# Two attentions on one core: the first step's scores moved into the projections' last turn, and a pair of maxima moved inside each output product

## The chip, the cores and the metric

One Trainium2 chip, one core of it. The number that counts is the device time of one execution in microseconds (us); a kernel's time is the median of its runs. The core has five engines that work side by side and meet through semaphores: TensorE (PE in the profile, with its weight loads shown apart as PEld), VectorE (DVE), ScalarE (ACT), GpSimd (POOL) and SyncE (SP, which here only issues DMAs).

## The reference: what is computed

Two multi-head attentions over a sequence of 2048 with 576 channels, 32 heads of 18 channels, each with its own input and weights. A attends to 8 earlier positions at a stride of 2; B is full softmax attention. Both end in a 576 x 576 output product, and the two results stand side by side.

```python
def _A_ref(x, wqkv, wo):
    qkv = (x @ wqkv).reshape(B, S, 3, H, Dh).transpose(2, 0, 3, 1, 4)
    q, k, v = qkv[0], qkv[1], qkv[2]
    idx = pos[:, None] - (jnp.arange(8) * 2)[None, :]          # masked where negative
    logits = einsum("bhsd,bhswd->bhsw", q, k[:, :, idx]) * Dh ** -0.5
    o = einsum("bhsw,bhswd->bhsd", softmax(logits), v[:, :, idx])
    return o.transpose(0, 2, 1, 3).reshape(B, S, D) @ wo
def _B_ref(x, wqkv, wo):
    q, k, v = ...                                              # as above
    p = softmax(einsum("bhqd,bhkd->bhqk", q, k) * Dh ** -0.5)
    return einsum("bhqk,bhkd->bhqd", p, v).transpose(0, 2, 1, 3).reshape(B, S, D) @ wo
return concatenate([_A_ref(...), _B_ref(...)], axis=-1)
```

## The kernel before, in words

**Products in two halves.** Products are made of float32r operands split into a high and a low part, three matmuls for one product. Most matmuls have at most 64 rows, so TensorE runs them in two halves of its array: the helper functions call the halves `r = 0` and `r = 1`, and the code alternates between them so that two matmuls run side by side.

**The projections** (up to about 423 us in the trace). After the first ones, which are written out by hand, `stream` (it ends in the matmul of L304) takes a list of 128-row products. It works in *turns*: one turn issues half of two products, lays some matmuls of the *maxima* (below) between them, and ends with `slot()`, which advances a counter and runs whatever was put into the list `todo` for that turn: loads of x and of weight chunks (`get`, L394 to L403), their splitting (`put`, L405 to L412: a copy on ACT, a subtraction on POOL), and the opening and closing of memory pools. The last 14 weight chunks are those of A (`chunk`); chunk 3 is loaded and split in the turns that follow `third_rows` (L575). `leave_a` (L622) copies a finished product to `ohi` on ACT and stores it to DRAM (`da`).

**Maxima.** Softmax of B subtracts a row maximum that is put in as two extra rows of q. `maximum(r)` (L140 and following) issues one matmul of queries by keys (54 rows, 512 columns, L161) into a bank of the ring "else" and returns, or makes at once, a reduction on DVE (L168, one number per row). 64 such pieces make a block (one group of four heads by 512 queries); its last piece sets off `least`, `turn` (a small matmul with the identity, L180), `halve` and `place`, some steps later. The first `EARLY_PAIRS` pairs of pieces are laid into the projections, the rest into the steps.

**PSUM.** Seven banks are handed out in rings by `bank`: four for "scores", three for "else"; an eighth holds the accumulators `po`. Whoever takes a bank waits until its last reader is done.

**The steps** (the loop at the end, 512 of them). A step belongs to a group g, a block b of 512 queries and a tile kt of 128 keys. For each of the four heads `score` issues a 56-row, 512-column matmul (L676), lets `maximum` issue one piece for the other half where `positions` says so (three a step as a rule), exponentiates the bank on ACT into a tile `e` (L679, eight tiles in rotation from the pool `work`) and then calls the reduction. After the four heads `weigh` multiplies the *previous* step's four `e` by the values into `po` (L686, four column tiles at once). So step 0 has nothing to weigh, and the first `weigh` is that of step 1.

**Around the steps.** `due()` runs what was planned for the step in `agenda`: A's local attention on POOL (`local`, with DVE's two reductions over the window, L823 among them), loads, normalisation. When an output product is due, the list `inside` holds a function, and the loop calls it between two heads of that step. The function calls `beside(kind, ...)` (L951 to L959), which takes one "scores" bank and one "else" bank and issues 14 and 13 matmuls of 64 rows and 288 columns (15 and 15 in the last group), alternating between the halves; L890, L891 and L892, or L972 and L973, then read the two banks. After the fourth head of such a step, `spare_pair` issues one more maximum for each half, as long as pieces are left.

**Between the projections and the steps** (L656 to L667): the pools of the projections are closed; what `agenda` still holds is run; the pool `work` is opened in the room that came free; `po` is cleared on DVE. Only then comes step 0.

Of the kernel before, what the change touches and what calls it, by code (L numbers as in the profile page):

```python
# [7 lines left out]
F32 = mybir.dt.float32  # L8
# [31 lines left out]
EARLY = 2  # L40
EARLY_PAIRS = EARLY * NB * PIECES
AHEAD = 7
# [17 lines left out]
def two_attentions(ctx: ExitStack, tc, xa, wa, woa, xb, wb, wob, c_id, c_sel, out):  # L60
# [35 lines left out]
    do = dram.tile([2, NG - 1, 128, S], F32, name="do")  # L96

    ident = const.tile([128, 128], F32, name="ident")

# [115 lines left out]

    def spare_pair():
        if sum(given) + 2 <= NG * NB * PIECES * 2:
            maxima_pairs(1)

    def maxima_pairs(n):  # L220
        for _ in range(n):
            for f in [maximum(r) for r in range(2)]:
                f()

# [45 lines left out]

    def stream(products, most):

        where, ends = {}, {}
        for j in range(len(products)):  # L280
            first = j - j % 4
            turn = [((0, 0), (1, 1)), ((0, 2), (1, 3)), ((0, 1), (1, 0)), ((0, 3), (1, 2))][j % 4]
            both = []
            for r, k in turn:
                args, view, _ = products[first + k]
                if j % 4 < 2:
                    where[k] = view(bank("scores"))
                else:
                    assert sum(given) - ends[k] > 3
                parts = halves(r, *args)  # L290
                both.append([(where[k], *ab, j % 4 < 2 and i == 0, j % 4 > 1 and i == len(parts) - 1)
                             for i, ab in enumerate(parts)])
            n = most(j) - given[0]
            total = n + len(both[0])
            for r in range(2):
                for i in range(n):
                    both[r].insert((4 * i + 1 + 2 * r) * total // (4 * n), None)
            for pair in zip(*both):
                for r, p in enumerate(pair):
                    if p is None:  # L300
                        maximum(r)()
                    else:
                        ps, a, b, start, stop = p
                        nc.tensor.matmul(ps, a, b, start=start, stop=stop)  # L304
# [16 lines left out]
    with (tc.tile_pool(name="x", bufs=1, side="right") as xp,  # L321
          tc.tile_pool(name="a0", bufs=1, side="right") as a0):

        early = ExitStack()
        first_pool = early.enter_context(tc.tile_pool(name="first", bufs=1))

        def raw(spare):
            if spare == "more":
                return more_room.tile([128, 512], F32, name="more", bufs=5)
            if spare:  # L330
                return first_pool.tile([128, 512], F32, name="first", bufs=16)
            return xp.tile([128, 512], F32, name="raw", bufs=5)

# [56 lines left out]
        def chunk(c):  # L390
# [5 lines left out]
            def get():  # L396
                t[0] = xp.tile([128, 512], F32, name="raw", bufs=5)
                load(ap(t[0], (n, 4), (1, n)), rows(wa[0, 128 * c], (3 * D, 128), (128 * 3 * D, 4), (1, n)))

            def get_last():  # L400
                t[1] = xp.tile([128, 512], F32, name="raw", bufs=5)
                for r in range(2):
                    load(t[1][64 * r : 64 * r + 64, :n], wa[512:, 128 * c : 128 * c + n])  # L403
# [20 lines left out]
        if True:  # L424
# [26 lines left out]

            zeros = xp.tile([128, 512], F32, name="ohi", bufs=4)
            nc.vector.memset(zeros, 0.0)
# [119 lines left out]
            wa_room = ExitStack()  # L573

            def third_rows():  # L575

                nonlocal wp
                odd.close()
                qkv.close()
                wp = wa_room.enter_context(tc.tile_pool(name="wa", bufs=1, side="right", reuse_waits="tile"))  # L580
                late = ctx.enter_context(tc.tile_pool(name="late", bufs=1, reuse_waits="tile"))
                make_set(late, 2)
# [46 lines left out]
            for t in order[:4]:  # L629
# [3 lines left out]
                slot()  # L633
            ring = "else"
            work_list = []
            for t in order[4:]:
# [23 lines left out]
        step = 0  # L660
# [4 lines left out]
    ring = "else"  # L665
    po = p_po.tile([128, 512], F32, name="po")
    nc.vector.memset(po, 0.0)  # L667

    def score(g, b, kt, h, also):

        assert (g, b) in placed
        qs, ks = sets[g % 3]
        p, r = divmod(h, 2)
        ps = bank("scores")
        at = slice(64 * r, 64 * r + 56)
        nc.tensor.matmul(ps, ks[at, p, 128 * kt : 128 * kt + 128], qs[at, b, p], start=True, stop=True)  # L676
        reduce = maximum(1 - r) if also else None
        e = work.tile([128, 512], F32, name="e", bufs=8)
        nc.scalar.activation(e, ps, AF.Exp, scale=SCALE)  # L679
        if reduce:  # L680
            reduce()
        return e

    def weigh(g, b, kt, es):
# [266 lines left out]
    def beside(kind, *both):  # L951

        sums_ = [bank(k)[:, :288] for k in (kind, None)]
        last = max(len(t) for t in both) - 1
        for i in range(last + 1):
            for r in range(2):
                if i < len(both[r]):
                    nc.tensor.matmul(sums_[r], *both[r][i], start=i == 0, stop=i == len(both[r]) - 1)  # L958
        return sums_  # L959
# [86 lines left out]

    ready = []
    early = sum(given)
# [13 lines left out]
    def positions(n):  # L1062
# [6 lines left out]
        return range(4) if n > 3 else (0, 1) if n == 2 else ()  # L1069

    while step < ALL:
        n, kt = divmod(step, NT)
        g, b = divmod(n, NB)
        places = positions(min(4 if behind() > 0 else 3, total - sum(given)))
        es, pair = [], False
        for h in range(4):

            if inside and h == (3 if 3 in places else 2):
                inside.pop(0)()
                pair = True  # L1080
# [42 lines left out]
```

## Time and profile before

| | us |
|---|---|
| median of the runs (lowest to highest) | 1691.18 (1690.31 to 1694.31) |
| the profiled execution, its own time | 1694.23 |
| its span in the profile | 1692.5 |
| PE busy | 1677.1 |
| DVE busy | 1408.5 |
| ACT busy | 1224.8 |
| POOL busy | 999.9 |

Busy times are unions of an engine's instructions. The ends of matmuls are modelled in the profile, so starts are what is to be read on PE. A profile row of a timeline merges instructions of one kind that follow each other: its first number is the first one's start, its second the length of all, and "x" how many there are. A `weigh` shows as eight matmuls, two for each of the four. "L161 PE MATMUL" is a maximum, "L676 PE MATMUL" a score, "L304" a projection, "L958" an output product.

### The profile page before, as it was taken

What the parts mean: (1) busy time and instruction counts of PE and PEld (TensorE: products, weight loads), DVE (VectorE), ACT (ScalarE), POOL (GpSimd) and SP (SyncE); (2) the same over time, 40 slices, a digit from 0 to 9 for tenths busy, and PEclk for the clock granted to TensorE, in tenths of its full rate; (3) what the DMA queues carried; (4) which work ended last, traced back from release to release, by engine and by line L of the source; (5) the groups of instructions that cost most, each with busy time, mean ns of one, the idle gap of its engine ahead of it and who ended that gap; (6) DMA issues with size and microseconds to landing.
All of it is one profiled execution on the core that took longest, in us unless ns stands there. A gap on an engine that the chain in (4) does not pass through costs nothing.

```text
span 1692.5 us, 33707 instructions
## 1 busy us (share of the span) xinstructions
PE 1677.1 (99%) x12994; PEld 928.2 (55%) x12994; DVE 1408.5 (83%) x2318; ACT 1224.8 (72%) x2420; POOL 999.9 (59%) x842
## 2 busy tenths in 40 slices
PE   9999999999999999999999999999999999999998
PEld 7998788887333444344344444444444444444665
DVE  5199999999889988888988888888888888888433
ACT  6323521221899988988988988988988988988444
POOL 2306732110286996995984996985995997812010
PEclk9999999999999999999999999999999999999999
DMA  8938855431624536165247128227526222134101
GB/s 250 244 99 223 245 152 139 129 99 62 86 82 62 143 96 106 58 155 112 66 106 155 68 79 173 84 61 129 128 69 124 77 79 70 37 102 172 45 30 57
DMA packets 186082, 188.37 MB, mean 111 GB/s; under 512 B 114832, under 2 KB 129936, under 8 KB 184192
## 3 DMA queue, kind: packets, MB, share of 16 engines
q1 hardware_dynamic: 181056, 174.66, 40.0%
q0 software_dynamic: 4032, 10.63, 3.0%
q8 instruction: 102, 1.67, 0.4%
q10 hardware_dynamic: 832, 0.92, 0.2%
q14 instruction: 60, 0.49, 0.1%
HBM read 113.30 MB, written 88.12 MB: 119 GB/s over the span
## 4 chain that ended last, share of the span: by engine, by line
PE 93%; DMA 3%; POOL 1%; DVE 1%; issue 1%; ACT 0%; SPq 0%; POOLq 0%; DVEq 0%; ACTq 0%
PE po L686 30%; PE bank L676 23%; PE bank L161 15%; PE bank L304 12%; PE bank L958 7%; PE bank L244 4%; DMA raw<-xa 1%; DMA dqk<-ohi 1%; PE bank L944 1%; POOL xlo L350 0%; DVE mx L168 0%; PE bank L180 0%; DVE rec L737 0%; POOL olo L443 0%; DMA first<-xb 0%
## 5 line engine op out<-in xcount | busy, mean ns | idle before, releaser
L168 DVE TENSOR_REDUCE mx<-bank 128x1 f32<-128x512 f32 x2048 | 1288.8, 684 | 144.8 <-PE bank L161 128.0
L679 ACT ACTIVATE e<-bank 128x512 f32<-128x512 f32 x2048 | 1061.6, 610 | 133.6 <-PE bank L676 60.0
L161 PE MATMUL bank<-ks,qs 54*128 54x512 f32 x2048 | 754.3, 424 | 5.1 <-DVE mx L168 1.6
L676 PE MATMUL bank<-qs,ks 56*128 56x512 f32 x2048 | 583.7, 426 | 0.5 <-ACT e L679 0.5
L676 PEld LDWEIGHTS bank<-qs,ks 56*128 56x128 f32 x2048 | 327.1, 186 | 433.3 <-ACT e L679 394.7
L686 PE MATMUL po<-e,v 128*19 128x512 f32 x4096 | 542.6, 601 | 0.0
L161 PEld LDWEIGHTS bank<-ks,qs 54*128 54x128 f32 x2048 | 342.2, 185 | 43.9 <-DVE part L891 14.3
L809 POOL TENSOR_TENSOR pr<-aq,akv 128x1024 f32<-128x1024 f32 x72 | 158.1, 2200 | 30.2 <-DMA akv<-dpart 28.0
L686 PEld LDWEIGHTS po<-e,v 128*19 128x19 f32 x4096 | 69.8, 97 | 179.1 <-issue 168.8
L846 POOL TENSOR_TENSOR pr<-lg,akv 128x1024 f32<-128x1024 f32 x72 | 158.2, 2198 | 0.3
L813 POOL TENSOR_TENSOR pr<-pr 128x1024 f32<-128x1024 f32 x64 | 152.5, 2382 | 5.0
L624 ACT ACTIVATE ohi<-bank 128x512 f32<-128x512 f32 (+1 forms) x56 | 30.5, 595 | 152.7 <-issue 114.4
L304 PE MATMUL bank<-xlo,ahi 64*128 64x512 f32 (+1 forms) x448 | 121.9, 392 | 0.3
L304 PE MATMUL bank<-xhi,alo 64*128 64x512 f32 (+1 forms) x448 | 119.0, 390 | 0.0
L304 PE MATMUL bank<-xhi,ahi 64*128 64x512 f32 (+1 forms) x448 | 115.2, 392 | 0.0
L847 POOL TENSOR_TENSOR pr<-pr 128x512 f32<-128x512 f32 x72 | 92.4, 1283 | 5.7
L892 POOL TENSOR_TENSOR y<-y,part 128x288 f32<-128x288 f32 x32 | 25.6, 800 | 111.9 <-ACT y L890 95.8
L443 POOL TENSOR_TENSOR olo<-olo,ohi 128x512 fp32r<-128x512 f32 x36 | 46.2, 1297 | 69.2 <-ACT ohi L442 66.6
L350 POOL TENSOR_TENSOR alo<-raw,ahi 128x512 fp32r<-128x512 f32 (+1 forms) x14 | 17.6, 1256 | 115.9 <-ACT ahi L349 115.9
L304 PEld LDWEIGHTS bank<-xlo,ahi 64*128 64x128 f32 (+1 forms) x448 | 68.2, 182 | 9.3 <-POOL xlo L350 1.2
L304 PEld LDWEIGHTS bank<-xhi,alo 64*128 64x128 f32 (+1 forms) x448 | 65.9, 182 | 8.9
L304 PEld LDWEIGHTS bank<-xhi,ahi 64*128 64x128 f32 (+1 forms) x448 | 61.8, 181 | 10.1 <-issue 1.1
(194 smaller groups left out, 1825.6 us busy)
## 6 DMA issues: line engine op xcount, KB each, us to landing
do<-n SPq DMA_DIRECT2D x28, 512.0 KB
da<-ohi SPq DMA_DIRECT2D x52, 256.0 KB
dpart<-da SPq DMA_DIRECT2D x16, 702.0 KB
akv<-dpart SPq DMA_DIRECT2D x16, 702.0 KB
out<-y SPq DMA_DIRECT2D x32, 288.0 KB
qs<-dqk SPq DMA_DIRECT2D x30, 288.0 KB
ks<-dqk SPq DMA_DIRECT2D x30, 288.0 KB
at<-dao SPq DMA_DIRECT2D x64, 128.0 KB
```

The source lines that it names most:

```text
L161: nc.tensor.matmul(ps, qs[at, b, p, 128 * t : 128 * t + 128], ks[at, p, 512 * k : 512 * k + 512], start=True, stop=True)
L168: nc.vector.tensor_reduce(mx[:, r, p, t, k : k + 1], ps, axis=AX.X, op=ALU.max)
L244: nc.tensor.matmul(ps, a, b, start=c == i == 0, stop=c == 4 and i == 1)
L304: nc.tensor.matmul(ps, a, b, start=start, stop=stop)
L676: nc.tensor.matmul(ps, ks[at, p, 128 * kt : 128 * kt + 128], qs[at, b, p], start=True, stop=True)
L679: nc.scalar.activation(e, ps, AF.Exp, scale=SCALE)
L686: nc.tensor.matmul(po[32 * i : 32 * i + 19], vs[g][:, kt, 19 * i : 19 * i + 19], es[i], start=kt == 0, stop=kt == NT - 1)
L809: nc.gpsimd.tensor_mul(pr, ap(st["q"][:, 2 * c], (SUB, 2), (0, W), (1, SUB)), window(st["k"], c))
L813: nc.gpsimd.tensor_add(st["pr"], st["pr"], pr)
L846: nc.gpsimd.tensor_mul(at, ap(st["lg"], (0, 2), (SUB, W), (1, SUB)), window(st["v"], c))
L847: nc.gpsimd.tensor_add(at[:, :, :4], at[:, :, :4], at[:, :, 4:])
L958: nc.tensor.matmul(sums_[r], *both[r][i], start=i == 0, stop=i == len(both[r]) - 1)
```

## The change

It has two main parts and what they need.

1. *Step 0's scores in the projections' last turn.* `score` moves up and `stream` gets a third argument: for its last turn, two score matmuls for each half, which are laid in ahead of that turn's maxima, between the product matmuls; these four scores take banks of the ring "else", without maxima of their own. Their exponentials are thus issued on ACT ahead of the last two `leave_a` copies. The loop starts at step 1 with the four tiles in `ready`. `EARLY_PAIRS` grows by 2.
2. *Rooms.* A tile `e` is wanted while the projections still hold their pools. The buffers `raw` move from the pool `xp` into a pool of their own (`rows`), which `third_rows` closes and opens again in another place (`rows2`); after the last weight chunk `first_room` closes it for good and opens the pool `es` with six tiles `e`. Two more stay in `work`; the rotation is of eight as before. Because of the new place, chunk 3 is loaded and split two turns later. The first `zeros` are a tile `raw` instead of `ohi`. `po` is taken at the start and cleared ahead of `stream`.
3. *What `agenda` still holds* after the projections isn't run at once any more, but moved on to the steps, at its distance.
4. *The pair of maxima of an output product.* `spare_pair` goes. `beside` puts a maximum of half 0 after the fourth matmul of that half, and one of half 1 after the tenth of that half. After the product it turns the ring "else" on by one, past the bank that the product itself used.

```diff
-EARLY_PAIRS = EARLY * NB * PIECES
+EARLY_PAIRS = EARLY * NB * PIECES + 2
...
+    def score(g, b, kt, h, also, kind="scores"):
...
+        ps = bank(kind)
...
+        counted[0] += 1
+        early = counted[0] % 8 < 6
+        e = (e_room if early else work).tile([128, 512], F32, name="e", bufs=6 if early else 2)
+        nc.scalar.activation(e, ps, AF.Exp, scale=SCALE)
...
     def stream(products, most, last):
...
             n = most(j) - given[0]
+            others = last if j == len(products) - 1 else ([], [])
+            n += len(others[0])
...
                     if p is None:
-                        maximum(r)()
+                        (others[r].pop(0) if others[r] else maximum(r))()
...
+            def first_room():
+
+                nonlocal e_room
+                raw_room.close()
+                e_room = ctx.enter_context(tc.tile_pool(name="es", bufs=1, reuse_waits="tile"))
...
-                at(n - 2, *ws[k][1])
                 if k == 3:
                     at(n, third_rows)
-                at(n, ws[k][2][0])
-                at(n + (k > 2), ws[k][2][1])
+                at(n - 2 if k != 3 else n, *ws[k][1])
+                at(n if k != 3 else n + 2, ws[k][2][0])
+                at(n if k == 2 else n + 1 if k > 3 else n + 3, ws[k][2][1])
+            at(90, first_room)
...
+            es = []
...
             stream(work_list, lambda j: 2 * (j + 1) if j < NT - 4 else
-                   few + (EARLY_PAIRS - few) * (j - NT + 5) // turns)
+                   few + (EARLY_PAIRS - few) * (j - NT + 5) // turns,
+                   [[lambda h=h: es.append(score(0, 0, 0, h, False, "else")) for h in (r, r + 2)] for r in range(2)])
         wa_room.close()
-        while agenda:
-            step += 1
-            due()
+
+        over, agenda = agenda, defaultdict(list)
+        for n, fs in over.items():
+            plan(n - step, [(0, f) for f in fs])
...
     def beside(kind, *both):
 
         sums_ = [bank(k)[:, :288] for k in (kind, None)]
-        last = max(len(t) for t in both) - 1
-        for i in range(last + 1):
+        turns = [[(sums_[r], *ab, i == 0, i == len(t) - 1) for i, ab in enumerate(t)] for r, t in enumerate(both)]
+        pair = kind and sum(given) + 2 <= NG * NB * PIECES * 2
+        if pair:
+
             for r in range(2):
-                if i < len(both[r]):
-                    nc.tensor.matmul(sums_[r], *both[r][i], start=i == 0, stop=i == len(both[r]) - 1)
+                turns[r].insert(4 + 6 * r, None)
+        for i in range(max(map(len, turns))):
+            for r in range(2):
+                if i < len(turns[r]):
+                    if turns[r][i]:
+                        ps, a, b, start, stop = turns[r][i]
+                        nc.tensor.matmul(ps, a, b, start=start, stop=stop)
+                    else:
+                        maximum(r)()
+        if pair:
+
+            rings["else"].append(rings["else"].pop(0))
         return sums_
...
-    ready = []
+    ready = [(0, 0, 0, es)]
...
+    due()
+    step += 1
     while step < ALL:
...
-        if pair:
-            spare_pair()
```

More of the change, by code (lines that the diff above doesn't have):

```diff
@@ L96, in two_attentions @@
     do = dram.tile([2, NG - 1, 128, S], F32, name="do")
+    po = p_po.tile([128, 512], F32, name="po")
     ident = const.tile([128, 128], F32, name="ident")
@@ L214, in maximum @@
         return lambda: reduce(ps, *piece)
[L216 to L223, printed above, removed]
+    e_room = None
+    counted = [-1]
+    def score(g, b, kt, h, also, kind="scores"):
+        assert (g, b) in placed
+        qs, ks = sets[g % 3]
+        p, r = divmod(h, 2)
+        ps = bank(kind)
+        at = slice(64 * r, 64 * r + 56)
+        nc.tensor.matmul(ps, ks[at, p, 128 * kt : 128 * kt + 128], qs[at, b, p], start=True, stop=True)
+        reduce = maximum(1 - r) if also else None
+        counted[0] += 1
+        early = counted[0] % 8 < 6
+        e = (e_room if early else work).tile([128, 512], F32, name="e", bufs=6 if early else 2)
+        nc.scalar.activation(e, ps, AF.Exp, scale=SCALE)
+        if reduce:
+            reduce()
+        return e
     vs = {}
@@ L269, in slot, with stream @@
             do_all(todo.popleft())
-    def stream(products, most):
+    def stream(products, most, last):
         where, ends = {}, {}
@@ L322, in two_attentions @@
           tc.tile_pool(name="a0", bufs=1, side="right") as a0):
+        raw_room = ExitStack()
+        rp = raw_room.enter_context(tc.tile_pool(name="rows", bufs=1, side="right"))
         early = ExitStack()
@@ L331, in raw @@
                 return first_pool.tile([128, 512], F32, name="first", bufs=16)
-            return xp.tile([128, 512], F32, name="raw", bufs=5)
+            return rp.tile([128, 512], F32, name="raw", bufs=5)
         def staged(src, cols, dims, into, spare=False):
@@ L396, in get @@
             def get():
-                t[0] = xp.tile([128, 512], F32, name="raw", bufs=5)
+                t[0] = rp.tile([128, 512], F32, name="raw", bufs=5)
                 load(ap(t[0], (n, 4), (1, n)), rows(wa[0, 128 * c], (3 * D, 128), (128 * 3 * D, 4), (1, n)))
             def get_last():
-                t[1] = xp.tile([128, 512], F32, name="raw", bufs=5)
+                t[1] = rp.tile([128, 512], F32, name="raw", bufs=5)
                 for r in range(2):
@@ L449, in leave @@
                         at += n
-            zeros = xp.tile([128, 512], F32, name="ohi", bufs=4)
+            zeros = rp.tile([128, 512], F32, name="raw", bufs=5)
             nc.vector.memset(zeros, 0.0)
@@ L634, in two_attentions @@
             ring = "else"
+            nc.vector.memset(po, 0.0)
             work_list = []
@@ L665, in two_attentions @@
     ring = "else"
[L666 to L682, printed above, removed]
     def weigh(g, b, kt, es):
@@ L1074, in two_attentions @@
         places = positions(min(4 if behind() > 0 else 3, total - sum(given)))
-        es, pair = [], False
+        es = []
         for h in range(4):
```

5 lines of the change are left out of this document (3 added, 2 removed).

## The prediction

> **What bounds the kernel now.** I read the page first.
>
> ```profile
> span 1692.5 us, 33707 instructions
> ...
> PE 1677.1 (99%) x12994; PEld 928.2 (55%) x12994; DVE 1408.5 (83%) x2318; ACT 1224.8 (72%) x2420; POOL 999.9 (59%) x842
> ...
> PE 93%; DMA 3%; POOL 1%; DVE 1%; issue 1%; ACT 0%; SPq 0%; POOLq 0%; DVEq 0%; ACTq 0%
> ```
>
> PE carries 93% of the chain that ends last, so time is won only where PE stands or runs badly paired; nothing here removes a matmul. A busy share of 99% hides that, since the ends of matmuls are modelled. So I read starts, in the timeline of PE, at the two places that the diff touches. First the end of the projections, with DVE and ACT beside it:
>
> ```profile
> 422.51 0.40 PE L304 MATMUL bank<-xhl,ahh 64*64 64x512 f32 x2
> 423.85 0.39 PE L180 MATMUL bank<-ident,m 128*16 128x128 f32 x2 [0.94 <-DVE m L174]
> 424.18 0.49 PE L676 MATMUL bank<-qs,ks 56*128 56x512 f32 x1
> ...
> 429.05 1.91 PE L686 MATMUL po<-e,v 128*19 128x512 f32 x8
> ...
> 436.02 1.05 PE L686 MATMUL po<-e,v 128*19 128x512 f32 x8
> ...
> 438.14 1.05 PE L686 MATMUL po<-e,v 128*19 128x512 f32 x8
> ```
> ```profile
> 425.13 4.20 DVE L168 TENSOR_REDUCE mx<-bank 128x1 f32<-128x512 f32 x7
> ```
> ```profile
> 426.70 3.54 ACT L679 ACTIVATE e<-bank 128x512 f32<-128x512 f32 x7 [1.40 <-DMA da<-ohi]
> ```
> ```profile
> 421.45:424.87 3.42, 2.48 (x21) 1.45 (x19) 2.74 (x7) 1.24 (x3) 0.19 (x1) 1.00 0.28 60
> 424.87:428.28 3.41, 2.56 (x12) 0.94 (x8) 3.41 (x7) 2.01 (x5) 0.54 (x2) 1.00 0.34 71
> 428.28:435.11 6.83, 6.83 (x28) 2.15 (x28) 2.98 (x5) 4.02 (x8) 0.00 (x0) 0.50 0.81 147
> 1018.79:1022.20 3.41, 2.72 (x15) 1.20 (x15) 3.41 (x6) 2.89 (x7) 2.74 (x3) 1.00 1.03 228
> 1022.20:1025.61 3.41, 3.41 (x21) 1.96 (x15) 2.04 (x4) 1.70 (x4) 0.00 (x0) 0.50 1.30 100
> ```
>
> From the last product matmul (422.51) to the fourth `weigh` (438.14) pass 15.63 us. An undisturbed step takes 2.12 (436.02 to 438.14). The windows show part of the reason (after the length come busy time and count of PE, PEld, DVE, ACT, POOL, then the granted clock): a thin window (424.87, 12 matmuls) is followed by 6.83 us at a clock of 0.50, which costs 6.83 / 2 = 3.4. The rest is that step 0 has nothing to weigh and that its exponentials wait 1.40 for a store. The same fall of the clock stands at 1022.20.
>
> Then the output products. Two of them, one of each kind that occurs, from `weigh` to `weigh`, PE and DVE:
>
> ```profile
> 625.83 1.05 PE L686 MATMUL po<-e,v 128*19 128x512 f32 x8
> 626.82 0.50 PE L676 MATMUL bank<-qs,ks 56*128 56x512 f32 x1
> 627.16 0.39 PE L676 MATMUL bank<-qs,ks 56*128 56x512 f32 x1
> 627.39 0.43 PE L958 MATMUL bank<-wohi,at 64*128 64x288 f32 x4
> ...
> 629.49 0.85 PE L161 MATMUL bank<-ks,qs 54*128 54x512 f32 x2
> 630.27 0.63 PE L686 MATMUL po<-e,v 128*19 128x512 f32 x4
> ```
> ```profile
> 627.39 1.29 DVE L168 TENSOR_REDUCE mx<-bank 128x1 f32<-128x512 f32 x2 [0.24 <-PE bank L161]
> 629.33 0.46 DVE L891 COPY part<-bank 128x288 f32<-128x288 f32 x1 [0.65 <-PE bank L958]
> ```
> ```profile
> 639.30 1.05 PE L686 MATMUL po<-e,v 128*19 128x512 f32 x8
> ...
> 640.63 0.62 PE L676 MATMUL bank<-qs,ks 56*128 56x512 f32 x2
> 640.86 0.53 PE L958 MATMUL bank<-wohi,at 64*128 64x288 f32 x3
> ...
> 642.58 0.39 PE L676 MATMUL bank<-qs,ks 56*128 56x512 f32 x1
> 642.68 0.29 PE L958 MATMUL bank<-wohi,ahl 64*128 64x288 f32 x1
> 642.81 0.29 PE L958 MATMUL bank<-wolo,ahl 64*128 64x288 f32 x1
> 642.94 1.11 PE L161 MATMUL bank<-ks,qs 54*128 54x512 f32 x3
> 643.98 0.63 PE L686 MATMUL po<-e,v 128*19 128x512 f32 x4
> ```
> ```profile
> 640.85 1.29 DVE L168 TENSOR_REDUCE mx<-bank 128x1 f32<-128x512 f32 x2 [0.47 <-PE bank L161]
> ```
>
> Kind A calls the product before its third head, kind B before its fourth. In both the spare pair stands last, and its second maximum takes the "else" bank that the product itself has just used: it starts only after the copy `part` (629.33 + 0.46 = 629.79). In A the pair's first maximum is at 629.49, and `weigh` begins at 630.27, 0.78 later, where one slot of 0.23 (627.16 to 627.39) and a change to `weigh` of 0.10 would do. Meanwhile DVE has stood 0.65 during the product. That is what part 4 of the change is about.
>
> **The change part by part.** The sum is made against the profiled execution, 1694.23 (span 1692.5 and 1.7 around it); the median of the runs, 1691.18, is 3.05 lower.
>
> *The seam (parts 1 to 3).* Added to the last turn: two pairs of scores and, by the larger `EARLY_PAIRS`, two pairs of maxima, four slots of 0.23, 0.9. The four scores share three "else" banks with the maxima, so some wait for an exponential; seven of these took 3.54, 0.51 each, so four take 2.0 and the wait lies between 0 and 2.0 - 0.9 = 1.1. I take 0.8, because the scores stand first in the turn. After the last product follow step 1's scores with three maxima. PE alone needs 0.34 + 3 x 0.23 + 0.10 = 1.1; DVE, which here is queued up and makes a reduction in 0.60 (4.20 / 7), lets the last maximum through only after four or more of them, 2.4, and one slot and the change to `weigh` follow, 2.8. I take 2.8: DVE stood in such a queue at this place before. Then the identity's matmul, 0.33 (423.85 to 424.18), and three steps, 6.36. In all 0.9 + 0.8 + 2.8 + 0.33 + 6.36 = 11.2 against 15.63, so -4.4, if the clock stays at 1.00. It should: that stretch holds 17 matmuls of step 1, `weigh` and the identity in some 3.9 us, ahead of them a turn without gaps, and the window at 421.45 with 21 in 3.42 us had no fall behind it, those with 12 and 15 had. Bounds: with both windows slow again -1.0; without any wait for banks or DVE 0.9 + 1.1 + 0.33 + 6.36 = 8.7, -6.9.
>
> [...]
>
> What moves with it: the four copies and stores of the last turn come behind four exponentials on ACT (2.0); their next reader is the rearrangement of `da`, whose results POOL needs ten steps later, so nothing. The `place` loads pass behind the three `dpart` loads on SP; they belong to block 7, which is wanted more than 100 steps later. Chunk 3: its load goes past `third_rows` and two turns later.
>
> ```profile
> ACT ahi L349 <- DMA raw<-wa: 10.9, 8, 2.9
> ```
>
> Before, it is split four turns ahead of its use, after, two. A turn of A takes 3.6 (two halves of 13 or 14 slots and its maxima), so 7 us stand against ACT and POOL's few; I take 0. If the load waits for its new room, the end to the other side is that longest wait, 2.9. Clearing `po` ahead (0.48 on DVE) and the `zeros` cost nothing: DVE waits there for PE.
>
> *The products (part 4).* By hand, from the start of `weigh` in the two steps above, a slot of a product being 0.13 (642.68 to 642.81). B: half 0's third score follows the second by a slot of 0.23, starts at 640.86 with half 1's first product matmul, and ends at 1.79; four product matmuls to 2.31; the early maximum wants the bank of the step's first one, reduced at 640.85 + 0.69 = 641.54, the 0.69 being what two in a row (1.29) take beyond one's 0.60, and 0.06 later for the semaphore, 2.30: no wait; to 2.54, ten more matmuls to 3.85, the fourth head's maximum to 4.08, change 0.10: 4.18. Half 1 runs beside it and is done by then: in the rows half 1's score at 642.58 starts ahead of half 0's product matmuls at 642.68 and 642.81, though it stands behind them in the program, so the halves don't wait for each other. A: the product begins at 1.56, the early maximum stands at 2.08, but its bank comes at 627.39 + 0.69 + 0.06 - 625.83 = 2.31. All that follows in the program waits 0.23. Then 0.33 (an empty array takes 0.34 for its first slot, 626.82 to 627.16), ten matmuls 1.31, the third score 0.23, change 0.10: 4.28. The late maximum has its bank (0.60 after the early one's) without wait in both, and DVE reduces both while it stood idle before.
>
> ```profile
> 619.27:623.70 4.43, 4.43 (x45) 1.00 0.35 124
> ...
> sum 71.68, PE 71.30; mean PE 4.46
> ```
> ```profile
> 639.30:643.99 4.69, 4.69 (x46) 1.00 0.78 183
> ...
> sum 65.96, PE 65.73; mean PE 4.69
> ```
> ```profile
> sum 22.19, PE 20.88; mean PE 5.22
> ```
>
> Sixteen steps of kind A take 71.68 / 16 = 4.48, fourteen of B 65.96 / 14 = 4.71, four more 22.19 / 4 = 5.55 for waits of other origin as well. So A wins 16 x 0.20 = 3.2, B 14 x 0.53 = 7.4, the four at B's rate 2.1: -12.7. I take -12. Bounds: A nothing and B 0.3: -4; A's wait gone and B 0.6, the four 0.9: -18.
>
> *The rest.* Four pieces fewer in the steps: their cover is the steps' own slots; 0 to -0.9, taken as 0. Six of eight `e` in other rooms, the rotation the same: 0.
>
> Sum: -4.4 - 12 = -16.4, 1677.8 for the profiled execution. The median is lower by 3.05, which is nearly two slow windows (1.7 each) that other executions may lack, so that the seam gives them less; I take 1677 for the median.
>
> **The rivals.**
> *The clock falls again at the seam*, because the maxima there are still paced by DVE: seam -1.0, 1680. For it the 12 and 15 matmuls of the windows ahead of a fall, against it the 21.
> *Strict order.* If a matmul may not start before an earlier one of the other half, each mixed pair costs a full 0.23: A 4.48, B 4.2, products -9, 1680. The row at 642.58 speaks against it. [...]
> *The steps give it back.* A's pieces are planned by step, POOL works by time.
>
> ```profile
> 1018.29 1.07 DVE L823 TENSOR_REDUCE am<-lg 128x64 f32<-128x512 f32 x1 [1.27 <-POOL lg L816]
> ```
>
> Steps that come earlier let DVE wait longer here and PE behind it; eight such places, each late by up to 12 / 8 = 1.5, return most of the 12: 1686. Against it: POOL is 59% busy.
> *Slower: the early maximum holds the product.* Half of the program's next matmuls stand behind its wait. If DVE is one reduction (0.69) later than in my walk in all 34 steps, products cost 34 x 0.69 - 12 = +11.5, with the seam +7: 1698. It decides against the change from 0.63 us per step on. Against it: DVE's idle 0.65 in each product.
>
> **How the numbers follow.** My forecast 0.58, clock 0.14, strict order 0.08, given back 0.13, slower 0.07. About 0.3% (5 us: below 1686.1 or above 1696.3) can be told from no change. The first three are faster, and half of the fourth: 0.86; same 0.08; slower 0.06. The range 1671 to 1686 takes in -20 to -5: both seams, products from -4 on, and leaves out the slower case and part of the given-back one.
>
> **What would show it.** Right: the clock 1.00 from 415 to 440; 11 us from the last L304 to the fourth L686; no [DMA da<-ohi] ahead of an exponential; steps with products of 4.2 to 4.4; one L161 early and one late among L958, DVE without the gap of 0.65. Wrong: L161 inside the product with an idle time of DVE mx well over 0.2, a new 0.50 window, longer waits at `am`, or chunk 3 waiting for its load.

## The result and the profile after

The changed kernel takes 1677.95 us (median; 1674.56 to 1678.14), the kernel before, run beside it, 1690.49. The ratio is 0.992 with a 95% interval of 0.9907 to 0.9932: 0.8% less time. 1677 was predicted, in a range of 1671 to 1686. The profiled execution took 1677.95 as well, with a span of 1676.2; against that of before, 1694.23, it is 16.3 shorter. Executions of one kernel differ by several us (the kernel before by 6.7 in 23 runs); part of that is how long they ran at half clock (the one of 1695.27 has a mean granted clock of 0.996, the one of 1688.55 of 0.998). In the trace of before the falls to 0.50 at 428.28 and 1022.20 last 6.83 and 3.41; half of that is their estimated cost, 1.7 for each 3.41, and each 3.41 is called a window of half clock. Below, what a run saves against the kernel before is worked out from its ratio, which need not be that of the two medians; against the changed kernel it is the difference of the medians.

From the page of the changed kernel: PE has the same 12994 matmuls and carries 89% of the chain, no longer 93%.

```profile
span 1676.2 us, 33705 instructions
...
PE 1664.2 (99%) x12994; PEld 922.9 (55%) x12994; DVE 1410.6 (84%) x2318; ACT 1223.3 (73%) x2420; POOL 998.6 (60%) x842
...
PE 89%; POOL 6%; SPq 2%; DVE 1%; DMA 1%; issue 1%; ACT 0%; POOLq 0%; ACTq 0%; DVEq 0%
```

In the changed kernel's lines L320 is a projection, L227 a score, L162 a maximum, L700 `weigh`, L979 an output product, L169 a reduction and L233 an exponential. First the seam in its timeline, PE, then ACT, then DVE, and the windows (after the length: busy time and count of PE, PEld, DVE, ACT, POOL, then the granted clock):

```profile
364.59 0.39 PE L320 MATMUL bank<-xhi,alo 64*128 64x512 f32 x1
...
419.74 0.50 PE L227 MATMUL bank<-qs,ks 56*128 56x512 f32 x1
...
420.23 0.50 PE L162 MATMUL bank<-ks,qs 54*128 54x512 f32 x1
...
420.71 0.50 PE L162 MATMUL bank<-ks,qs 54*128 54x512 f32 x1
...
422.70 0.39 PE L320 MATMUL bank<-xhl,ahh 64*64 64x512 f32 x1
...
425.42 1.05 PE L700 MATMUL po<-e,v 128*19 128x512 f32 x8
426.29 0.38 PE L181 MATMUL bank<-ident,m 128*16 128x128 f32 x2
...
427.74 1.05 PE L700 MATMUL po<-e,v 128*19 128x512 f32 x8
...
431.98 1.05 PE L700 MATMUL po<-e,v 128*19 128x512 f32 x8
```
```profile
419.11 2.03 ACT L233 ACTIVATE e<-bank 128x512 f32<-128x512 f32 x4
...
424.15 2.03 ACT L233 ACTIVATE e<-bank 128x512 f32<-128x512 f32 x4
```
```profile
422.23 4.27 DVE L169 TENSOR_REDUCE mx<-bank 128x1 f32<-128x512 f32 x7
```
```profile
420.00:440.00 20.00, 19.90 (x136) 8.57 (x134) 17.40 (x30) 16.68 (x34) 0.73 (x2) 1.00 0.90 112
```

From the last projection matmul to the fourth `weigh` pass 431.98 - 422.70 = 9.28 where there were 15.63. The clock stays at 1.00, no exponential waits for a store, and three maxima paced by DVE (4.27 / 7 = 0.61 each) put the first `weigh` 2.72 behind the last product. In the last turn, scores and maxima stand for the exponentials of their banks (419.74, 420.23, 420.71: 0.48 apart, 2.03 / 4 = 0.51 each).

Then the two kinds of product, A (613.14 to 617.52) and B (633.06 to 637.35), PE, with DVE of A between them:

```profile
613.14 1.05 PE L700 MATMUL po<-e,v 128*19 128x512 f32 x8
...
615.09 0.29 PE L979 MATMUL bank<-wohi,at 64*128 64x288 f32 x2
615.44 0.49 PE L162 MATMUL bank<-ks,qs 54*128 54x512 f32 x1
615.44 0.40 PE L979 MATMUL bank<-wohi,at 64*128 64x288 f32 x1
...
616.97 0.39 PE L162 MATMUL bank<-ks,qs 54*128 54x512 f32 x1
617.09 0.49 PE L227 MATMUL bank<-qs,ks 56*128 56x512 f32 x2
617.52 1.05 PE L700 MATMUL po<-e,v 128*19 128x512 f32 x8
```
```profile
614.69 2.79 DVE L169 TENSOR_REDUCE mx<-bank 128x1 f32<-128x512 f32 x4 [0.23 <-PE bank L162]
617.40 0.45 DVE L905 COPY part<-bank 128x288 f32<-128x288 f32 x1
```
```profile
633.06 1.05 PE L700 MATMUL po<-e,v 128*19 128x512 f32 x8
...
635.39 0.47 PE L162 MATMUL bank<-ks,qs 54*128 54x512 f32 x1
...
637.02 0.40 PE L162 MATMUL bank<-ks,qs 54*128 54x512 f32 x1
637.35 1.05 PE L700 MATMUL po<-e,v 128*19 128x512 f32 x8
```

DVE works through the product. In A the early maximum starts at 615.44, 2.30 after `weigh`; the slot before it, of the 0.13 measured before (642.68 to 642.81), ended at 615.09 + 0.13 = 615.22, and the next product matmul starts at 615.44 as well, so both halves stood for 0.22.

One place became worse, at step 255. DVE waits 2.84 for GpSimd there (1.27 before), the window over this wait holds 12 matmuls, and behind it stand two windows at half clock (one before):

```profile
1009.66 1.03 DVE L837 TENSOR_REDUCE am<-lg 128x64 f32<-128x512 f32 x1 [2.84 <-POOL lg L830]
```
```profile
1007.40:1010.82 3.42, 1.70 (x12) 0.32 (x9) 1.16 (x2) 2.65 (x6) 2.96 (x4) 1.00 0.67 170
1010.84:1017.67 6.83, 6.32 (x27) 3.60 (x29) 4.71 (x8) 3.10 (x6) 2.43 (x2) 0.50 1.26 137
```

The 16.3 come from these places (starts of projection matmuls and of `weigh` in both traces, differences after minus before):

| stretch | us |
|---|---|
| up to the 400th last projection matmul (365.74 to 364.59) | -1.15 |
| from there to the fourth weigh (72.40 to 67.39) | -5.01 |
| 16 products of kind A (71.68 to 70.30) | -1.38 |
| 14 products of kind B (65.96 to 60.00) | -5.96 |
| the four other products (22.20 to 19.78) | -2.42 |
| seven steps with A's normaliser `as` (22.04 to 20.04) | -2.00 |
| step 255, the wait for `am` (4.04 to 6.07) | +2.03 |
| other steps | -0.01 |
| from the last weigh to the end of the span (16.81 to 16.43) | -0.38 |

The normaliser's steps were in no step of the prediction. DVE spends 1.04 + 0.55 there on `as`, one or two steps behind a product. One place of the seven, of before and then of after:

```profile
650.75 1.88 DVE L168 TENSOR_REDUCE mx<-bank 128x1 f32<-128x512 f32 x3
652.55 1.04 DVE L823 TENSOR_REDUCE as<-lg 128x64 f32<-128x512 f32 x1
```
```profile
644.52 0.68 DVE L169 TENSOR_REDUCE mx<-bank 128x1 f32<-128x512 f32 x1
645.12 1.07 DVE L837 TENSOR_REDUCE as<-lg 128x64 f32<-128x512 f32 x1
```

One reduction stands right ahead of `as`, not three, and `as` begins 0.96 after its `weigh` (644.16) where it began 1.23 after it (651.32).

### The profile page after: what moved, and what is told of

Read it like the earlier page. It is cut to its first block, busy times and chain, and to the rows that moved or that the text cites. A ratio compares the mean times of both kernels' runs of the same rounds, so it can differ in the third digit from the quotient of the medians.

```text
span 1676.2 us, 33705 instructions
## 1 busy us (share of the span) xinstructions
PE 1664.2 (99%) x12994; PEld 922.9 (55%) x12994; DVE 1410.6 (84%) x2318; ACT 1223.3 (73%) x2420; POOL 998.6 (60%) x842
## 4 chain that ended last, share of the span: by engine, by line
PE 89%; POOL 6%; SPq 2%; DVE 1%; DMA 1%; issue 1%; ACT 0%; POOLq 0%; ACTq 0%; DVEq 0%
PE po L700 27%; PE bank L227 21%; PE bank L320 14%; PE bank L162 14%; PE bank L979 7%; PE bank L257 4%; SPq L146 1%; POOL pr L823 1%; POOL pr L860 1%; POOL pr L827 1%; DVE mx L169 1%; POOL pr L861 1%; DMA rec<-drec 1%; PE bank L958 1%; PE bank L181 0%
## 5 line engine op out<-in xcount | busy, mean ns | idle before, releaser
L169 DVE TENSOR_REDUCE mx<-bank 128x1 f32<-128x512 f32 x2048 | 1294.4, 685 | 154.1 <-PE bank L162 132.0
L233 ACT ACTIVATE e<-bank 128x512 f32<-128x512 f32 x2048 | 1060.4, 610 | 108.6 <-PE bank L227 57.1
L162 PE MATMUL bank<-ks,qs 54*128 54x512 f32 x2048 | 757.6, 424 | 5.0 <-DVE mx L169 2.7
L227 PE MATMUL bank<-qs,ks 56*128 56x512 f32 x2048 | 582.9, 425 | 0.0
L227 PEld LDWEIGHTS bank<-qs,ks 56*128 56x128 f32 x2048 | 327.2, 186 | 430.7 <-ACT e L233 403.1
L700 PE MATMUL po<-e,v 128*19 128x512 f32 x4096 | 541.0, 600 | 0.0
L162 PEld LDWEIGHTS bank<-ks,qs 54*128 54x128 f32 x2048 | 342.8, 185 | 34.2 <-DVE mx L169 16.8
L700 PEld LDWEIGHTS po<-e,v 128*19 128x19 f32 x4096 | 69.8, 97 | 181.7 <-issue 170.7
L320 PE MATMUL bank<-xlo,ahi 64*128 64x512 f32 (+1 forms) x448 | 121.8, 391 | 0.1
L320 PE MATMUL bank<-xhi,alo 64*128 64x512 f32 (+1 forms) x448 | 118.6, 390 | 0.0
L320 PE MATMUL bank<-xhi,ahi 64*128 64x512 f32 (+1 forms) x448 | 115.2, 392 | 0.0
L320 PEld LDWEIGHTS bank<-xlo,ahi 64*128 64x128 f32 (+1 forms) x448 | 68.1, 182 | 9.4 <-POOL xlo L368 0.5
L320 PEld LDWEIGHTS bank<-xhi,alo 64*128 64x128 f32 (+1 forms) x448 | 65.4, 182 | 9.1
L979 PE MATMUL bank<-wohi,at 64*128 64x288 f32 x512 | 68.9, 301 | 0.0
```

What stands on the lines that cost most here:

```text
L162: nc.tensor.matmul(ps, qs[at, b, p, 128 * t : 128 * t + 128], ks[at, p, 512 * k : 512 * k + 512], start=True, stop=True)
L169: nc.vector.tensor_reduce(mx[:, r, p, t, k : k + 1], ps, axis=AX.X, op=ALU.max)
L700: nc.tensor.matmul(po[32 * i : 32 * i + 19], vs[g][:, kt, 19 * i : 19 * i + 19], es[i], start=kt == 0, stop=kt == NT - 1)
```

## The experiments

**The two parts apart.** Part 4 alone, on the kernel before:

```diff
         sums_ = [bank(k)[:, :288] for k in (kind, None)]
...
+                turns[r].insert(4 + 6 * r, None)
...
+            rings["else"].append(rings["else"].pop(0))
...
-        if pair:
-            spare_pair()
```

> The kernel before with part 4 alone (the pair of maxima inside the product, the turn of the ring, no spare pair). My theory now, from the step lengths of the two traces: 34 product steps give 9.8 (kind A 1.4, kind B 6.0, the four others 2.4), the eight steps with the normaliser of A (the reduction 'as') give 2.1 more, and the fifth wait of VectorE for 'am' takes back up to 2.0; so 10 to 12 less than the kernel before, 1678.5 to 1680.5 where that is 1690.5. As predicted before the result: 12 less from products, nothing from other steps, 1678.5, with kind A at 4.28 instead of the 4.38 to 4.41 seen. Rival: the part gains little by itself and the seam made the rest possible: 1684 or more.

Measured 1682.55, ratio 0.9951 (0.9938 to 0.9964): 8.3 less (0.0049 x 1692). In its profile A takes 4.39, B 4.28 and the normaliser's seven steps 20.02, all as in the changed kernel, so the products' gain doesn't need the seam. That is short of the 10 to 12, though the interval, 6.1 to 10.5 less, just touches them. In the profile the wait for `am` grew still more: step 255 took 6.78, 2.7 more than before.

```profile
1013.31 1.03 DVE L823 TENSOR_REDUCE am<-lg 128x64 f32<-128x512 f32 x1 [3.57 <-POOL lg L816]
```

Parts 1 to 3 alone, the changed kernel with the old `beside` and `spare_pair`:

```diff
-                turns[r].insert(4 + 6 * r, None)
...
-            rings["else"].append(rings["else"].pop(0))
...
+        if pair:
+            spare_pair()
```

> The changed kernel with the old products and the spare pair: parts 1 to 3 alone. My theory: 4.8 from the seam (of the last turn, its added slots and the steps up to the fourth weigh) and 1.8 in the projections at 191 and 224 us, so 6.6 less than before, 1684. As predicted: 4.4 from the seam and nothing in the projections, 1686. Rival: the clock falls at the seam as it did before: 1.0 plus 1.8, 1687.5.

Measured 1686.42, ratio 0.9972 (0.9964 to 0.9981): 4.7 less. 0.9951 x 0.9972 = 0.9923, so the two parts add up to the whole. The 1.8 that I had claimed for the projections did not come.

**The projections' 1.8.** In the profile of before, PE stands 1.3 at 191 us for a copy into `olo`; in that of after it doesn't. I suspected the tile of zeros, which moves the rotation of the `ohi` buffers by one.

```diff
-            zeros = xp.tile([128, 512], F32, name="ohi", bufs=4)
+            zeros = xp.tile([128, 512], F32, name="raw", bufs=5)
```

> The kernel before with one line changed: the first tile of zeros is a buffer 'raw' instead of 'ohi', so that both rotations stand one further on. Theory: this alone shortens ScalarE's wait for the store of 'ohi' at 177 to 185 us (8.2 before, 4.6 after the change) and with it removes TensorE's waits at 191 and 224: 1.3 to 1.8 less than before, 1689. Rival: the later place of chunk 3 and the rooms did it, and this line does nothing: 1690.5, with the wait of 1.3 for 'olo' still there.

Measured 1691.90, ratio 1.0003 (0.9993 to 1.0014), and the wait is still there, in the waits of PE between 150 and 240 us:

```profile
PE bank L304 <- ACT olo L441: 1.1, 1, 1.1
```

The theory fell. The wait belongs to no kernel: the profile of part 4 alone has the same projections as before and lacks it, and two profiles further down have the changed kernel's projections and show it with 1.3 and 1.5. It comes and goes between executions, so the -1.15 of the table can't be counted as a gain of the change.

**The wait for am.** In the changed kernel, the fifth local attention alone makes its maximum two steps later:

```diff
             plan[36 + 5 * c // 2] = lambda c=c: weighted(c)
+        if j == 4:
+            del plan[29], plan[30]
+            plan.update({31: most, 32: lower, 34: exponents, 35: total, 36: lambda: (share(), weighted(0))})
```

> The changed kernel, in which the fifth of the eight local attentions (and it alone) makes its maximum two steps later, and what follows on it up to the first weighted sum is put one or two steps later as well. Theory: VectorE waits 2.8 there for GpSimd, TensorE stands behind it, and the thin window is followed by two windows of 3.4 at half clock; with the maximum two steps (4.2) later wait and fall go, which gives 3.4 for the clock and 1 to 2 for the wait: 4.4 to 5.4 less than the changed kernel, 1673. Rival: the clock falls there for another reason (it also fell in the kernel before, at nearly the same place): only the wait goes, 1676 to 1677, with a window of 0.50 between 1005 and 1025 us. Second rival: what is put later makes GpSimd late for something else, 1678 or more.

Measured 1673.57 (1673.38 to 1673.71), 4.4 less than the changed kernel; ratio to before 0.9894 (0.9881 to 0.9907). DVE's timeline and a window over the place:

```profile
1009.12 1.89 DVE L169 TENSOR_REDUCE mx<-bank 128x1 f32<-128x512 f32 x3 [0.24 <-PE bank L162]
1010.92 1.06 DVE L837 TENSOR_REDUCE am<-lg 128x64 f32<-128x512 f32 x1
```
```profile
1004.00:1022.00 18.00, 17.68 (x154) 9.34 (x150) 16.27 (x27) 14.49 (x30) 11.02 (x10) 1.00 1.02 172
```

Wait and fall are gone together: step 255 takes 2.12 (6.07), step 256 4.92 (6.01). The same edit in the kernel before:

> The kernel before with the later maximum of the fifth local attention alone. Theory (a window thinned by the wait for 'am' makes the clock fall): 1.9 of the step in which it waits (4.04 instead of 2.12) and about 1 of the half clock in the next one go, so 2.5 to 4.5 less than before, and no window of 0.50 between 1005 and 1030 us. Rival: the fall at 1022 in the kernel before comes from the large step that follows (the last before a new group, 6.24), not from the wait: no more than 2 less, the fall stays.

1688.39, ratio 0.9983 (0.9975 to 0.9992), 2.9 less; steps 255 and 256 take 2.13 and 4.83 (4.04 and 6.24), and the window from 1000 to 1030 has a clock of 1.00. So the fall at 1022 in the kernel before went with this wait too.

**The turn of the ring.**

```diff
-        if pair:
-
-            rings["else"].append(rings["else"].pop(0))
         return sums_
```

> The changed kernel without the turn of the ring 'else' behind a product. Theory: the next head's maximum then takes the bank of the product and stands until VectorE has copied 'part', which comes behind four reductions: in the profile of the changed kernel that copy ends at 617.85 (kind A, maximum at 616.97) and 637.79 (kind B, maximum at 637.02), so 0.8 to 0.95 more in each of 34 steps, 27 to 32 in all: about 1707 where the changed kernel takes 1678. Rival: the turn is of no account, because the pair inside the product is what counts: 1678 to 1680.

1704.98 (1704.92 to 1705.02), 27 more than the changed kernel; kind A takes 5.45, B 5.20. The next head's maximum stands for the copy:

```profile
617.67 0.50 PE L162 MATMUL bank<-ks,qs 54*128 54x512 f32 x1 [0.42 <-DVE part L905]
```
```profile
617.17 0.45 DVE L905 COPY part<-bank 128x288 f32<-128x288 f32 x1
```

A pair inside the product without the turn is slower than the kernel before. The pieces' place and the order of their banks are one change.

**Where the early maximum stands.** First later, after the sixth matmul:

```diff
-                turns[r].insert(4 + 6 * r, None)
+                turns[r].insert(6 + 4 * r, None)
```

> The changed kernel with the early maximum after the sixth instead of the fourth matmul of its half. Theory: in kind A it waits 0.22 for its bank (it starts at 615.44, the matmul before it ended its slot at 615.22), and everything behind it waits too; two matmuls later (0.26) it does not. Kind A then takes 4.17 to 4.25 instead of 4.39, kind B stays at 4.28: 2.4 to 3.5 less, 1674.5 to 1675.5 where the changed kernel takes 1678. Rival: kind A is bounded by VectorE (four reductions and a copy), not by this wait: no change.

1675.72 (1673.98 to 1677.12); ratio to before 0.9907 (0.9891 to 0.9924), which overlaps that of the changed kernel. The steps in its profile are clear: A 4.25 (4.39), B 4.21 (4.29), 3.7 less over the 34. That execution has the wait for `olo`, of 1.3. Then earlier, after the second (`2 + 8 * r`):

> The changed kernel with the early maximum after the second instead of the fourth matmul of its half. Theory (a maximum inside the product that waits for its bank holds everything behind it): the piece is called for 0.26 earlier and its bank comes free at the same time, so in kind A the wait grows from 0.22 to 0.48, in kind B from nothing to 0.25: 16 x 0.26 + 18 x 0.25 = 8.7 more, 1685 to 1687 where the changed kernel takes 1678, A at 4.65 and B at 4.53. Rival: the product's other matmuls go past a maximum that waits; then the steps stay as they are, 1678.

1685.89; ratio 0.9969 (0.9957 to 0.9982). A takes 4.66 and B 4.55, as worked out. The early maximum of A in its profile:

```profile
613.87 0.43 PE L979 MATMUL bank<-wohi,at 64*128 64x288 f32 x4
614.62 0.50 PE L162 MATMUL bank<-ks,qs 54*128 54x512 f32 x1 [0.31 <-DVE mx L169]
614.62 0.39 PE L979 MATMUL bank<-wolo,at 64*128 64x288 f32 x1
```

Nothing of either half starts between 614.01, the second pair of L979 (613.87 + 0.43 - 0.29), and 614.62: for 0.61, where a slot is 0.13, the maximum that waited held all that the program has behind it.

Both edits that helped, the early maximum at six and the later `am`, in the changed kernel:

> The changed kernel with both: the early maximum after the sixth matmul and the later maximum of the fifth local attention. Theory: the two add, 4.4 and 2.4 to 3.5 less than the changed kernel: 1670 to 1671. Rival: only the later maximum counts, 1673.5.

1671.84 (1669.39 to 1672.55), ratio to before 0.9883 (0.9867 to 0.9900): the lowest of this study. Beside the later `am` alone (0.9894) the intervals overlap. Its steps are 3.7 shorter from the fourth `weigh` to the last, but its profiled execution entered them 2.5 later, with a wait of 1.5 for `olo`.

**What made the seam shorter.** The changed kernel without the early scores; step 0 is the loop's again:

```diff
-                   [[lambda h=h: es.append(score(0, 0, 0, h, False, "else")) for h in (r, r + 2)] for r in range(2)])
+                   [[], []])
...
-    ready = [(0, 0, 0, es)]
+    ready = []
...
-    due()
-    step += 1
```

> The changed kernel without part 1's early scores: step 0 is the loop's again, the projections' last turn holds maxima only; rooms, agenda and the two more pairs of maxima stay. Theory: the scores alone carry the seam's gain, rooms and agenda are worth nothing: 4 to 5 more than the changed kernel, 1682 to 1683, with 14 to 15.6 from the last projection matmul to the fourth weigh (9.3 in the changed kernel), and a window of 0.50 there, because the window ahead of it is thin again. Rival: what was moved on by the agenda (the identity's matmul at once behind the projections) is what kept the windows full: 1678 to 1680, and the clock stays at 1.00.

1676.57 (1675.81 to 1680.15), ratio to before 0.9921 (0.9904 to 0.9937): no slower than with the scores (1677.95). Both forecasts of the time were out. The clock did fall in the profiled execution, for one window, behind one with 18 matmuls:

```profile
423.94:427.36 3.42, 3.02 (x18) 1.25 (x17) 3.42 (x7) 3.42 (x8) 0.00 (x0) 1.00 0.43 78
427.36:430.77 3.41, 3.41 (x18) 1.43 (x17) 1.46 (x4) 1.79 (x4) 0.60 (x2) 0.50 0.99 193
```

Next, the agenda's rest also run at once again, so that only the rooms, the two more pairs and the earlier clearing of `po` are left of the seam's parts; and, the other way, the agenda's rest alone moved in the kernel before:

```diff
-        over, agenda = agenda, defaultdict(list)
-        for n, fs in over.items():
-            plan(n - step, [(0, f) for f in fs])
+        while agenda:
+            step += 1
+            due()
```

> The changed kernel without the early scores and with the agenda's rest run at once again, as before the change: of the seam's parts only the rooms and the two more pairs of maxima are left. Measure: from the 400th last projection matmul to the fourth weigh (72.4, 71.0, 71.9 and 72.4 us in the four profiles with the old seam, 67.4 with the changed one, 68.9 without the early scores, with one window of half clock in it, which is 1.7). Theory: the rooms carry it, since the first exponentials no longer wait for stores of 'ohi' (1.4 before) and VectorE need not clear 'po' there; 68.9 to 69.5, and about 1676 to 1679 as a whole. Rival: the agenda's rest carries it: 71 to 72, and 1679 to 1682.

> The kernel before with the agenda's rest moved on to the steps, nothing else. Same measure. Theory (rooms carry it): the identity's matmul and its wait for VectorE (0.9 + 0.3) go to a step that has to make room for 0.2 to 0.3, so at most 1 less than the old seam: 71 to 72. Rival (the agenda's rest carries it): 69 to 70, and no half clock there.

With rooms alone 1675.97 (1674.91 to 1677.28), ratio to before 0.9915 (0.9898 to 0.9931); with the agenda alone 1692.06, ratio 1.0007 (0.9995 to 1.0019). ACT at the seam, first with the agenda alone, then with the rooms alone, and of the latter the PE rows and the window that answers to the thin one:

```profile
424.10 0.59 ACT L679 ACTIVATE e<-bank 128x512 f32<-128x512 f32 x1
427.14 3.53 ACT L679 ACTIVATE e<-bank 128x512 f32<-128x512 f32 x7 [2.46 <-DMA da<-ohi]
```
```profile
422.35 14.06 ACT L233 ACTIVATE e<-bank 128x512 f32<-128x512 f32 x27
```
```profile
420.90 0.40 PE L320 MATMUL bank<-xhl,ahh 64*64 64x512 f32 x2
421.23 0.39 PE L181 MATMUL bank<-ident,m 128*16 128x128 f32 x2
...
424.87 1.05 PE L700 MATMUL po<-e,v 128*19 128x512 f32 x8
...
431.21 1.05 PE L700 MATMUL po<-e,v 128*19 128x512 f32 x8
```
```profile
420.79:424.21 3.42, 3.42 (x20) 1.65 (x16) 3.42 (x8) 2.83 (x6) 0.73 (x2) 1.00 0.31 66
```

The seam in all profiles, from the starts of matmuls; the sum is what a kernel pays:

| seam | 400th last to last projection | to the fourth weigh | sum | windows at 0.50 |
|---|---|---|---|---|
| before | 56.78 | 15.62 | 72.40 | 2 |
| same code in three other profiles | 56.77 to 56.78 | 14.26 to 15.60 | 71.04 to 72.37 | 1 or 2 |
| agenda alone | 56.77 | 14.54 | 71.31 | 1 |
| changed | 58.11 | 9.28 | 67.39 | 0 |
| changed code, six other profiles | 58.10 to 58.11 | 9.25 to 9.28 | 67.35 to 67.39 | 0 |
| no early scores | 56.77 | 12.12 | 68.89 | 1 |
| rooms alone | 56.77 | 10.31 | 67.08 | 0 |

In the profile with the rooms alone the whole gain is there. Without the half clock (an estimated 1.7 a window) the stretch behind the last projection is 11.7 to 12.8 long with the old rooms, and 10.3 or 10.4 with the new; so 1.3 to 2.5 are the rooms' by themselves, and the rest is half clock that did not come. The two more pairs of maxima and the earlier clearing of `po` were not tried apart from the rooms, and the rooms alone have one profile. What the trace does show is that the exponentials' wait for the store is there with the old rooms (2.46) and gone with the new. The early scores then save 10.31 - 9.28 = 1.03 behind the last projection and cost 58.11 - 56.77 = 1.34 ahead of it. Whether they guard against a fall of the clock stays open: none in seven profiles with them, one in two without. In the two kernels without them the heads' maxima also fall the other way round: steps that were of kind A are of kind B and the reverse, with 4.41 for A and 4.28 for B. Behind the fourth `weigh` they take 1226.4 and 1226.9 in all where the changed kernel takes 1227.8, so little of their time comes from there.

## Why the prediction was right, and where it was not

*The seam* was put at -4.4 and gave -5.0. Its terms: added slots and bank waits 0.9 + 0.8 = 1.7, measured 1.34; last product to first `weigh` 2.8, measured 2.72, with DVE as the pace; identity and three steps 0.33 + 6.36 = 6.69, measured 431.98 - 425.42 = 6.56. The clock stayed at 1.00. But the reasons given were wrong in two places. The step that failed is "Six of eight `e` in other rooms, the rotation the same: 0": the rooms, with what came with them, are what let the exponentials go without the store (1.40 in the rows that the prediction itself quotes, 2.46 with the agenda alone). Moving the scores saved 1.03 and cost 1.34, and the times show no gain of it. The sum held because it was walked along the changed kernel, in which the rooms are already free. And the clock was forecast from the number of matmuls in a window (21 safe, 12 and 15 not), which does not decide it, as the last section shows; that it stayed at 1.00 was forecast rightly for a reason that does not hold.

*The products* were put at -12 and gave -9.8: kind A -1.38 instead of -3.2, B -5.96 instead of -7.4, the four others -2.42 instead of -2.1. The early maximum's wait in A, 0.23, came as 0.22. What was mis-sized is A's end, 4.28 against 4.39. I walked half 0 only; in half 1 the late maximum (616.34), three last product matmuls, the third head's maximum (616.97) and, 0.23 later, the fourth score follow each other and end 0.11 behind half 0. B's 4.18 came as 4.29, and of that 0.08 goes when the early maximum stands two matmuls later: the 2.30 at which it was to stand and the 2.30 at which its bank was to be free left no room.

*The rest* was put at 0 and is 0 by accident: -2.0 in the normaliser's steps against +2.0 at step 255. The latter is the third rival, the steps giving it back, at one of its eight places, because GpSimd had no time to spare at that one alone (in the changed kernel it stands 19.3 in all waiting for DVE's `am` at the other seven). The wait there was 1.27 with the old products before the change, 1.68 with the new seam and the old products, and 2.84, 3.57 and 4.69 in the changed kernel, with part 4 alone and with the rooms alone. Without the turn of the ring, whose products are slower, there is no wait and step 255 takes 2.70.

*The other rivals.* The clock fell again, but at 1011 and not at the seam. The slower case, the early maximum holding the product, did occur, at a small price: with the early maximum at two nothing starts for 0.61 in the rows shown, and 0.26 of place cost 8 us. Strict order between the halves as a cost was not tried apart; at the two waits shown (0.22 at 615.44 and that of 0.61) neither half went past the maximum that waited.

That 1677.8 was forecast for the profiled execution and 1677.95 came is partly luck: seam 0.6 better, products 2.2 worse, 1.15 from an execution that entered the last projections earlier, 0.4 at the end.

## What to carry to other kernels

Where an engine starts late at a change of phase, look for the buffer it writes into before moving its work: here the rooms opened early, with two more pairs of maxima and an earlier clearing, gave all that the move of the first step was credited with. When work is put inside a product, walk every half of the array to its end, and give each bank that it takes half a slot more than the walk says (A's end came 0.11 behind it, half of 0.23); the order of the banks behind it was worth more here (27 us) than the place (8 us from the fourth matmul to the second). After any gain on the bounding engine, list the waits for engines that run by their own time, and move the one without slack: that was 4.4 us for three lines.

## What the runs showed of the hardware

The clock fell behind windows in which PE was far from idle, busy for 1.70 to 3.02 us in those shown. One at the seam, with the agenda alone, and what followed:

```profile
425.10:428.51 3.41, 1.81 (x7) 0.85 (x7) 2.49 (x5) 1.37 (x3) 0.00 (x0) 1.00 0.78 147
428.51:431.92 3.41, 3.41 (x15) 0.93 (x15) 1.16 (x3) 2.16 (x5) 0.00 (x0) 0.50 0.97 183
```

In the rows shown, falls followed windows of 3.41 or 3.42 us with 7, 12, 12, 15 and 18 matmuls (PE busy for 1.81 in the one with 7, for 3.02 in the one with 18), and none followed those with 20 and 21. But neither this number nor the busy time alone decides. In the profile with the other tile of zeros two windows hold 15 matmuls each:

```profile
905.07:908.48 3.41, 2.51 (x15) 0.87 (x15) 3.38 (x7) 2.17 (x4) 1.66 (x3) 1.00 1.43 136
423.79:427.20 3.41, 3.02 (x15) 1.63 (x13) 3.02 (x7) 2.77 (x7) 0.72 (x2) 1.00 0.37 79
```

Behind the first, the less busy one, the clock stayed at 1.00; behind the second it was 0.50 for two windows. With the early maximum at two DVE waited 1.88 for `am` at 1011.17, more than the 1.27 of before, yet the mean granted clock of that execution is 1.0 to three places, where a fall of 3.41 would take 0.001 from it. That the fall there goes with the wait is shown by moving it, in both kernels; what in a window decides stays open.

The two halves run a little apart: in the prediction's rows a score of half 1 starts at 642.58, 0.10 ahead of a product matmul of half 0 (642.68) that stands before it in the program. But the maximum that waited for its bank with the early maximum at two stopped both of them for the 0.61 up to 614.62.
